# Attention scores and slot reads in the `h` banks, two groups of tiled products a batch, and a new place for the loads and transposes of x

## Chip, cores and metric

The kernel runs on one core of one Trainium2 chip. The metric is the device time of one execution in microseconds (us); lower is better. A run counts as slow where it lies over 1.5% above the fastest of the same kernel, and ratios use fast runs alone.

## The reference, cut to what matters

```python
B, H, S, Ns, D = 8, 8, 512, 32, 64
scale = 1 / sqrt(D)
a     = softmax(scale * x @ state.T)       # per batch and head: [512, 32], over the slots
xread = a @ state
a2    = softmax(scale * state @ x.T)       # [32, 512], over the tokens
sread = a2 @ x
y     = concat([xread, sread], tokens)     # 544 tokens a batch, 512 features
h     = y @ w_in                           # 512 -> 2048
g     = s * relu(h)**2 + b
out   = g @ w_out                          # 2048 -> 512
```

## The kernel before

The kernel does two products more cleverly than the reference writes them. The input weights are folded through the state, M = state times w_in, so that h is one product of M with the softmax shares `a`. The second product, g times w_out, uses seven half-size products in place of eight, with sums of quarters of g (`token_sum`, tiles `s`) and of w_out (tiles `wd`).

Per batch, TensorE does 16 pairs of `h` matmuls (128x512) and 112 `o` matmuls (128x256, tiles oA, oB and oC). Between them stand the small products that prepare the next batch, in tiles of 64x32 or 128x32: `T` (the scores), `M` in four parts and `V` (the slot reads).

The softmax of batch b needs these steps in a row: x is loaded (`xn`), transposed by a DMA (`xT`), multiplied with the state (`T`), exponentiated on ScalarE (`E`), transposed by a DMA (`ET`), normalised on VectorE (`den`, `inv`, `aT`), and transposed back by a DMA (`a`). In batches before NDT the denominator comes from a TensorE product `D` instead. All DMA transposes are issued from one queue, SP, in order. The loads of x are issued from the GpSimd queue (POOL).

```python
    psA = ctx.enter_context(tc.tile_pool(name="psA", bufs=2, space=bass.MemoryType.PSUM))
    psH = ctx.enter_context(tc.tile_pool(name="psH", bufs=2, space=bass.MemoryType.PSUM))
    psO = ctx.enter_context(tc.tile_pool(name="psO", bufs=2, space=bass.MemoryType.PSUM))
    ...
    def att_xT_dma(b):
        xT = new_xT(b)
        nc.sync.dma_start_transpose(
            out=xT.rearrange("p h k t -> p (h k) t"),
            in_=xn[b].rearrange("p h c d -> p (h c d)"),
        )
    ...
    def att_T(b, gs):                      # scores: two att banks, then exponentials
        ...
        T = att_ps([P, 2, 512], FP32, f"T_{b}_{gs[0]}")
        ...                                # 16 tiled matmuls
    ...
    def pieces(s):                         # what is done beside product f of batch s
        nb = s + 1
        ...
            if s + 3 < B:
                at(13 if s == 2 else 2, lambda: load_x(s + 3))
            if s == 2:
                at(0, stT_dma)
            if nb < B:
                at(3, lambda: att_T(nb, [0, 1]))
                at(3, lambda: att_M(nb, 0, "act"))
                at(4, lambda: att_ET(nb))
                if s in (2, 3):
                    at(4, lambda: att_xT_dma(nb + 1))
                if s >= 3 and s + 3 < B:
                    at(13, lambda: att_xT_dma(s + 3))
                if nb < NDT:
                    at(5, lambda: att_D(nb, [0, 1]))
                else:
                    at(8, lambda: att_shares(nb))
                    at(9, lambda: att_a4_dma(nb))
                at(7, lambda: att_M(nb, 1, "act"))
                at(7, lambda: att_M(nb, 2, "act"))
            ...
            at(10, lambda: att_V(s))
            ...
            if nb < B:
                at(10, lambda: att_M(nb, 3, "act"))
```

The softmax here doesn't subtract the row's maximum and nothing guards it: scores larger than these inputs give would overflow.

## Time and profile before

| | before |
|---|---|
| median of 3 runs | 210.24 us (209.90 to 210.72) |
| span of the profiled run | 208.0 us |
| TensorE (PE) busy | 199.5 us, 96% |
| VectorE (DVE), ScalarE (ACT) busy | 78%, 60% |
| granted TensorE clock | 1.00 |
| batch 2, then batches 3 to 6 | 23.2 us, then 21.3 us each |

The median is the whole execution as timed; the span is what the profile sees of it. A batch runs from its first `h` product to the next batch's; the scores `T` that run in batch 4 prepare batch 5. TensorE is the bound, so the first question to a change is what it does to the length of a batch. The prediction shows the lines that carry this.

### The profile page before, as it was taken

The numbers are of one execution on the slowest core, as the hardware profiler recorded it, in microseconds if no ns is written. First come the engines' busy times: TensorE is split into PE (matmuls) and PEld (weight loads), VectorE is DVE, ScalarE is ACT, GpSimd is POOL, SyncE is SP. The second block draws the span as 40 slices with busy tenths as digits, with TensorE's granted clock in tenths as the row PEclk, the third lists the DMA queues.
The fourth block names the chain that finished last, engine by engine and source line by source line (L and its number), as shares of the span: only waits on it lengthen the run. The fifth ranks groups of instructions, "written<-read, shape, count | busy, mean of one in ns | idle before, by whom it ended". The sixth has DMA issues, their size and how long they took to land.

```text
span 208.0 us, 4757 instructions
## 1 busy us (share of the span) xinstructions
PE 199.5 (96%) x1947; PEld 129.4 (62%) x1947; DVE 162.1 (78%) x282; ACT 125.3 (60%) x218; POOL 37.6 (18%) x64
## 2 busy tenths in 40 slices
PE   7888999999899999999999999999999999999992
PEld 2433343445566676667666766676667777788882
DVE  1587825978769796899779977998799877895862
ACT  3678865698489557765776477656774544533100
POOL 5970001501110330123011201120111012100210
PEclk9999999999999999999999999999999999999999
DMA  5999996999947299979833915231324111110143
GB/s 183 225 202 206 207 191 104 179 181 174 266 52 153 72 194 123 124 163 185 127 103 67 196 52 102 54 107 54 101 29 132 50 54 50 54 50 0 54 145 111
DMA packets 45946, 25.35 MB, mean 122 GB/s; under 512 B 30884, under 2 KB 43940, under 8 KB 45924
## 3 DMA queue, kind: packets, MB, share of 16 engines
q0 software_dynamic: 15536, 16.19, 38.8%
q1 hardware_dynamic: 29588, 8.49, 23.8%
q10 hardware_dynamic: 800, 0.36, 0.7%
q8 instruction: 15, 0.25, 0.5%
q14 instruction: 7, 0.06, 0.1%
HBM read 17.33 MB, written 8.91 MB: 126 GB/s over the span
## 4 chain that ended last, share of the span: by engine, by line
PE 82%; DVE 6%; DMA 6%; ACT 4%; issue 1%; POOL 0%; SPq 0%; POOLq 0%
PE h L70 23%; PE oB L70 17%; PE oC L70 12%; PE oA L70 10%; PE o L70 6%; PE Mps L70 4%; DMA wi<-in_moe_w_in_dram 4%; PE h_sr L70 3%; DMA stT_all<-st 2%; ACT r L365 2%; DVE g L371 1%; PE T L70 1%; PE oB_sr L70 1%; PE V L70 1%; DVE M L298 1%; PE oA_sr L70 1%
## 5 line engine op out<-in xcount | busy, mean ns | idle before, releaser
L365 ACT ACTIVATE r<-h 128x512 f16<-128x512 f32 x126 | 74.4, 601 | 52.0 <-PE h L70 51.4
L70 PE MATMUL h<-a,M 128*128 128x512 f16 x256 | 75.0, 379 | 0.9 <-DVE M L298 0.6
L371 DVE TENSOR_TENSOR g<-r 128x1024 f16<-128x1024 f16 x64 | 44.1, 691 | 16.0 <-ACT r L365 15.8
L70 PEld LDWEIGHTS <-s 128*128 128x128 f16 x448 | 42.8, 98 | 19.3 <-issue 3.7
L70 PEld LDWEIGHTS <-g 128*128 128x128 f16 x400 | 38.0, 98 | 18.9 <-issue 2.9
L536 POOL DMA_DIRECT2D out_dram<-osb x27 | 18.2, 675 | 125.5 <-DVE osb L528 120.3
L70 PE MATMUL oB<-wd,s 128*128 128x256 f16 x224 | 32.7, 273 | 0.0
L70 PE MATMUL oA<-wo,g 128*128 128x256 f16 x224 | 31.6, 273 | 0.1
L70 PEld LDWEIGHTS <-M 128*128 128x128 f16 x256 | 24.6, 98 | 10.9 <-DVE M L298 1.6
L301 ACT CAST M<-Mps 128x1024 f16<-128x1024 f32 x27 | 26.8, 1017 | 1.4 <-PE Mps L70 0.8
L70 PE MATMUL oC<-wd,s 128*128 128x256 f16 x112 | 16.5, 273 | 0.0
L70 PE MATMUL o<-wo,g 128*128 128x512 f16 x64 | 16.3, 380 | 0.0
L70 PE MATMUL oB<-wd,g 128*128 128x256 f16 x112 | 15.9, 273 | 0.0
L70 PE MATMUL oC<-wo,s 128*128 128x256 f16 x112 | 15.3, 273 | 0.0
L365 ACT ACTIVATE r_sr<-h_sr 128x256 f16<-128x256 f32 x16 | 6.1, 382 | 8.4 <-PE h_sr L70 8.4
L227 ACT ACTIVATE E<-T 128x512 f16<-128x512 f32 x16 | 9.4, 596 | 1.2 <-PE T L70 1.1
L471 DVE TENSOR_TENSOR s<-s,g 128x1024 f16<-128x1024 f16 x14 | 9.7, 691 | 0.4
L70 PE MATMUL h_sr<-srdT,wi 128*128 128x256 f16 x64 | 9.6, 273 | 0.0
L465 DVE TENSOR_TENSOR s<-g 128x1024 f16<-128x1024 f16 x14 | 9.6, 685 | 0.0
L473 DVE TENSOR_TENSOR s<-g,s 128x1024 f16<-128x1024 f16 x14 | 9.6, 684 | 0.0
L469 DVE TENSOR_TENSOR s<-g,g 128x1024 f16<-128x1024 f16 x14 | 9.6, 683 | 0.0
L528 DVE SCALAR_TENSOR_TENSOR osb<-oC,s_bc,u 128x512 f32<-128x512 f32 x12 | 8.9, 746 | 0.5 <-PE oC L70 0.5
(102 smaller groups left out, 187.4 us busy)
## 6 DMA issues: line engine op xcount, KB each, us to landing
out_dram<-osb POOLq DMA_DIRECT2D x31, 256.0 KB, 2.8
xn<-in_x_dram POOLq DMA_DIRECT2D x7, 512.0 KB, 7.0
wi<-in_moe_w_in_dram POOLq DMA_DIRECT2D x4, 512.0 KB, 9.2
wo<-in_moe_w_out_dram POOLq DMA_DIRECT2D x4, 512.0 KB, 15.9
xf<-in_x_dram SPq DMA_DIRECT2D x2, 512.0 KB, 4.8
out_dram<-osb_sr SPq DMA_DIRECT2D x8, 32.0 KB, 1.6
out_dram<-osb_sr ACTq DMA_DIRECT2D x8, 32.0 KB, 1.7
out_dram<-osb_last SPq DMA_DIRECT2D x2, 128.0 KB, 1.9
```

The costliest lines, as they stand in the source:

```text
L70: return nc.tensor.matmul(out, lhsT, rhs, start=start, stop=stop, tile_position=tp, is_transpose=is_transpose, skip_group_check=True,)
L227: nc.scalar.activation(a["E"][:, g, :].rearrange("p (m t) -> p m t", m=2), T[:, :, 256 * i : 256 * i + 256], AF.Exp, scale=scale, accum_ou ...
L298: nc.vector.tensor_copy(dst[:, 0], two[0])
L301: nc.scalar.copy(dst, ps)
L365: nc.scalar.activation(r16[:, f % 2], hps, AF.Relu)
L371: nc.vector.tensor_mul(gt[:, f % 4 - 1 : f % 4 + 1], r16, r16)
L465: nc.vector.tensor_sub(o, a11, a21)
L469: nc.vector.tensor_add(o, a21, a22)
L471: nc.vector.tensor_sub(o, SQ[b, 1, j], a11)
L473: nc.vector.tensor_sub(o, a12, SQ[b, 2, j])
L528: nc.vector.scalar_tensor_tensor(osb, acc[bank], s_bc, add, ALU.mult, ALU.add)
L536: nc.gpsimd.dma_start(dst[j][:, :, n0 : n0 + NH], osb)
```

## The change

The intent is to save TensorE time at the edges of tiled products. Three insertions a batch become two: [M0, T, M1] before product 4 and [V, M2, M3] before product 10. For that, scores and slot reads move into the `h` banks, and the M copies wait behind a relu. The softmax normalised on VectorE (the transposed one) starts at batch 3, so one more batch does without `D`. The load of x comes first in a batch, and the transpose of x moves to product 9, behind the transpose of the shares. Slot scaling moves to ScalarE, the fourth sums to the next batch, and rows of `o` go ahead of `h` for products 4 to 12.

```diff
-    NST = 3
-    NDT = 4
+    NST = 5
+    NDT = 3
 ...
     def att_T(b, gs):
+        one_bank = b >= NDT
+        if one_bank:
+            Ts = [psH.tile([P, NG, S // 2], FP32, tag="h", name=f"T_{b}_{m}") for m in range(2)]
 ...
     def att_V(b):
-        ps = att_ps([P, NG, D], FP32, f"V_{b}")
+        if b >= NDT - 1:
+            ps = psH.tile([P, NG, D], FP32, tag="h", name=f"V_{b}")
 ...
-            if s + 3 < B:
-                at(13 if s == 2 else 2, lambda: load_x(s + 3))
-            if s == 2:
-                at(0, stT_dma)
+            if 2 < s < B - 2:
+                at(0, lambda: load_x(s + 2))
             if nb < B:
-                at(3, lambda: att_T(nb, [0, 1]))
-                at(3, lambda: att_M(nb, 0, "act"))
+                if nb < NST:
+                    at(0, lambda: att_stT(nb))
+                ahead(4, lambda: att_M(nb, 0, "later"))
+                ahead(4, lambda: att_T(nb, [0, 1]))
+                ahead(4, lambda: att_M(nb, 1, "later"))
                 at(4, lambda: att_ET(nb))
-                if s in (2, 3):
-                    at(4, lambda: att_xT_dma(nb + 1))
-                if s >= 3 and s + 3 < B:
-                    at(13, lambda: att_xT_dma(s + 3))
 ...
+                at(8, lambda: att_shares(nb))
+                at(9, lambda: att_a4_dma(nb))
+                if s == 3:
+                    at(9, stT_dma)
+                if nb + 1 < B:
+                    at(9, lambda: att_xT_dma(nb + 1))
 ...
-            at(10, lambda: att_V(s))
+            ahead(10, lambda: att_V(s))
+            if nb < B:
+                ahead(10, lambda: att_M(nb, 2, "later"))
+                ahead(10, lambda: att_M(nb, 3, "later"))
 ...
             for f in range(NKF):
+                for fn in todo_s.get((f, "ahead"), []):
+                    fn()
+                if s > 1 and 4 <= f < 13:
+                    for fn in items[f]:
+                        fn()
+                    items[f] = []
                 mm1_x(s, f)
```

More of the change, by code (lines that the diff above doesn't have):

```diff
@@ L210, in att_T @@
         a = A[b]
-        n = len(gs)
-        T = att_ps([P, 2, 512], FP32, f"T_{b}_{gs[0]}")
+        one_bank = b >= NDT
+        if one_bank:
+            Ts = [psH.tile([P, NG, S // 2], FP32, tag="h", name=f"T_{b}_{m}") for m in range(2)]
+        else:
+            T = att_ps([P, 2, 512], FP32, f"T_{b}_{gs[0]}")
+            Ts = [T[:, m, 0 : 256 * len(gs)].rearrange("p (g t) -> p g t", t=256) for m in range(2)]
         for q in range(NQ):
@@ L217, in att_T @@
                     mm(
-                        T[32 * q : 32 * q + 32, m, 256 * i : 256 * i + 256],
+                        Ts[m][32 * q : 32 * q + 32, i, :],
                         st_of(b, h, m),
@@ L224, in att_T @@
             a["E"] = apool.tile([P, NG, S], FP16, name=f"E_{b}", tag="E", bufs=3)
-            a["rs"] = apool.tile([P, NG], FP32, name=f"rs_{b}", tag="rs", bufs=4)
+            n = 2 * NG if one_bank else NG
+            a["rs"] = apool.tile([P, n], FP32, name=f"rs_{b}", tag="rs", bufs=4)
+        if one_bank:
+            for m in range(2):
+                for g in gs:
+                    nc.scalar.activation(
+                        a["E"][:, g, 256 * m : 256 * m + 256],
+                        Ts[m][:, g, :],
+                        AF.Exp,
+                        scale=scale,
+                        accum_out=a["rs"][:, NG * m + g : NG * m + g + 1],
+                    )
+            return
         for i, g in enumerate(gs):
@@ L277, in att_a4_dma, with copy_M @@
         )
+    def copy_M(dst, ps):
+        with tc.issue_after(G["relu"]):
+            nc.scalar.copy(dst, ps)
     def att_M(b, c, how):
@@ L296, in att_M @@
         dst = a["M"][:, :, FC * c : FC * c + FC]
-        if how == "split":
+        if how == "later":
+            a["M", c] = lambda: copy_M(dst, ps)
+        elif how == "split":
             nc.vector.tensor_copy(dst[:, 0], two[0])
@@ L309, in att_ET @@
         a["rq"] = apool.tile([P, NG], FP32, name=f"rq_{b}", tag="rq", bufs=4)
-        nc.vector.reciprocal(a["rq"], a["rs"])
+        rs = a["rs"]
+        if b >= NDT:
+            rs = apool.tile([P, NG], FP32, name=f"rt_{b}", tag="rt")
+            nc.vector.tensor_add(rs, a["rs"][:, 0:NG], a["rs"][:, NG : 2 * NG])
+        nc.vector.reciprocal(a["rq"], rs)
     def att_V(b):
         a = A[b]
-        ps = att_ps([P, NG, D], FP32, f"V_{b}")
+        if b >= NDT - 1:
+            ps = psH.tile([P, NG, D], FP32, tag="h", name=f"V_{b}")
+        else:
+            ps = att_ps([P, NG, D], FP32, f"V_{b}")
         for g in range(NG):
@@ L326, in att_V @@
         a["sr"] = apool.tile([P, NG, D], FP16, name=f"sr_{b}", tag="sr")
-        for g in range(NG):
-            nc.vector.tensor_scalar(a["sr"][:, g], ps[:, g], a["rq"][:, g : g + 1], None, ALU.mult)
+        with tc.issue_after(G["relu"]):
+            for g in range(NG):
+                nc.scalar.mul(a["sr"][:, g], ps[:, g], a["rq"][:, g : g + 1])
     def att_srT_dma(b):
@@ L365, in mm1_close @@
             nc.scalar.activation(r16[:, f % 2], hps, AF.Relu)
+            G["relu"] = nc.cur_bb.bb.instructions[-1]
         if f % 4 == 0:
@@ L756, in at, with ahead @@
                 out.setdefault(f, []).append(fn)
+            def ahead(f, fn):
+                out.setdefault((f, "ahead"), []).append(fn)
             if s == 1:
@@ L779, in pieces @@
                 return out
-            if s + 3 < B:
-                at(13 if s == 2 else 2, lambda: load_x(s + 3))
-            if s == 2:
-                at(0, stT_dma)
+            if 2 < s < B - 2:
+                at(0, lambda: load_x(s + 2))
             if nb < B:
-                at(3, lambda: att_T(nb, [0, 1]))
-                at(3, lambda: att_M(nb, 0, "act"))
-                at(4, lambda: att_ET(nb))
-                if s in (2, 3):
-                    at(4, lambda: att_xT_dma(nb + 1))
-                if s >= 3 and s + 3 < B:
-                    at(13, lambda: att_xT_dma(s + 3))
-                if nb < NDT:
-                    at(5, lambda: att_D(nb, [0, 1]))
-                else:
-                    at(8, lambda: att_shares(nb))
-                    at(9, lambda: att_a4_dma(nb))
-                at(7, lambda: att_M(nb, 1, "act"))
-                at(7, lambda: att_M(nb, 2, "act"))
+                if nb < NST:
[3 more added lines that the diff above has]
+                ahead(4, lambda: att_M(nb, 1, "later"))
+                at(4, lambda: att_ET(nb))
+                at(4, lambda: A[nb]["M", 0]())
+                at(6, lambda: A[nb]["M", 1]())
+                at(8, lambda: att_shares(nb))
[4 more added lines that the diff above has]
+                    at(9, lambda: att_xT_dma(nb + 1))
             if s == 2:
@@ L802, in pieces @@
                 at(12, lambda: att_srT_dma(1))
-            at(10, lambda: att_V(s))
+            ahead(10, lambda: att_V(s))
+            if nb < B:
+                ahead(10, lambda: att_M(nb, 2, "later"))
+                ahead(10, lambda: att_M(nb, 3, "later"))
+                at(10, lambda: A[nb]["M", 2]())
+                at(12, lambda: A[nb]["M", 3]())
             if s == last_b:
@@ L807, in pieces @@
                 at(12, lambda: att_srT_dma(s))
-            if nb < B:
-                at(10, lambda: att_M(nb, 3, "act"))
             if s == last_b:
@@ L832 @@
             for f in range(NKF):
+                for fn in todo_s.get((f, "ahead"), []):
[4 more added lines that the diff above has]
+                    items[f] = []
                 mm1_x(s, f)
-                if s == 2 and f in (8, 9):
+                if s > 1 and f in (4, 5):
                     with tc.issue_after(G["last"]):
-                        token_sum(1, 4, f - 8)
-                if s > 2 and f == 0:
-                    token_sum(s - 1, 4, 1)
+                        token_sum(s - 1, 4, f - 4)
                 if s in fast:
@@ L845 @@
                             token_sum(s, f - 12, 0)
-                    if s > 1 and f in (11, 12, 13):
-                        token_sum(s, (1, 2, 4)[f - 11], 0)
+                    if s > 1 and f in (11, 12):
+                        token_sum(s, f - 10, 0)
                     if f == 15:
@@ L866 @@
             mm1_sr(f)
-            if f == 5:
-                token_sum(last_b, 4, 1)
+            if f in (4, 5):
+                token_sum(last_b, 4, f - 4)
             if f in (5, 9):
```

## The prediction

> **What bounds the kernel now.** I read the page's busy table first, then the chain that ended last, then the table of stretches over single batches, then the timeline of TensorE inside one batch, then ScalarE and VectorE there. Busy table and the head of the chain:
>
> ```profile
> PE 199.5 (96%) x1947; PEld 129.4 (62%) x1947; DVE 162.1 (78%) x282; ACT 125.3 (60%) x218; POOL 37.6 (18%) x64
> ...
> PE 82%; DVE 6%; DMA 6%; ACT 4%; issue 1%; POOL 0%; SPq 0%; POOLq 0%
> ```
>
> TensorE is the bound: 96% busy and 82% of the chain; VectorE has a fifth of the span free, ScalarE two fifths. The granted clock is full throughout. So a change pays only where it shortens what TensorE issues or a gap in it. In the timeline the first product `h` of batches 2, 3, 4 and 5 starts at 52.26, 75.5, 96.8 and 118.04. Cut there, the table of stretches gives (length, then busy time of PE, PEld, DVE, ACT, POOL, with counts; clock, DMA share, GB/s):
>
> ```profile
> 52.26:75.48 23.22, 22.40 (x260) 14.89 (x258) 18.64 (x33) 16.04 (x26) 3.50 (x5) 1.00 0.64 135
> 75.48:96.76 21.28, 21.28 (x226) 14.59 (x225) 18.68 (x31) 14.18 (x25) 3.61 (x5) 1.00 1.03 154
> 96.76:118.04 21.28, 21.28 (x226) 14.59 (x224) 18.68 (x31) 14.18 (x25) 3.60 (x5) 1.00 0.65 127
> ```
>
> Batches 3 to 6 repeat every 21.28 us with no idle TensorE at all; batch 2 is 1.94 us longer and has 0.82 us idle. That repeat is one unit of 7 `o` products and 2 `h` products, 1.19 to 1.20 us, done 16 times (about 19.15 us), plus three insertions of tiled products. The timeline of batch 4/5 shows the three:
>
> ```profile
> 105.82 0.59 PE L70 MATMUL h<-a,M 128*128 128x512 f16 x2
> 106.35 0.63 PE L70 MATMUL Mps<-wi,stT_all 64*32 64x512 f16 x16
> 106.91 0.94 PE L70 MATMUL oC<-wd,s 128*128 128x256 f16 x7
> ...
> 110.07 0.59 PE L70 MATMUL h<-a,M 128*128 128x512 f16 x2
> 110.60 0.42 PE L70 MATMUL V<-xn,ET 128*32 128x64 f16 x32
> 110.95 0.41 PE L70 MATMUL Mps<-wi,stT_all 64*32 64x512 f16 x8
> 111.29 0.94 PE L70 MATMUL oB<-wd,g 128*128 128x256 f16 x7
> ...
> 121.63 0.59 PE L70 MATMUL h<-a,M 128*128 128x512 f16 x2
> 122.16 0.43 PE L70 MATMUL T<-xT,stT_all 64*32 64x256 f16 x16
> 122.38 0.42 PE L70 MATMUL Mps<-wi,stT_all 64*32 64x512 f16 x8
> 122.74 0.28 PE L70 MATMUL oB<-wd,s 128*128 128x256 f16 x1
> ```
>
> Starts matter here, not durations, which overlap. After an `h` pair the next full-array product normally starts 0.43 us after the pair's start. So the insertions cost 106.91-(105.82+0.43)=0.66, 111.29-110.50=0.79 and 122.74-122.06=0.68 us, in all 2.13; with 19.15 that is the 21.28. Eight M products or sixteen T products alone take 0.22 (122.16 to 122.38). So 0.66 is 2x0.21 of work plus 0.23 of entry and exit; 0.68 the same plus 0.25; V itself takes 0.35 and its insertion also some 0.23 at the edges. A switch into and out of tiled products costs a quarter of a microsecond.
>
> Batch 2's extra is visible too (bracket: idle before it and what ended it):
>
> ```profile
> 57.45 0.43 PE L70 MATMUL T<-xT,stT_all 64*32 64x256 f16 x16 [0.79 <-DMA stT_all<-st]
> 55.28 0.66 PEld L70 LDWEIGHTS <-s 128*128 128x128 f16 x7 [0.51 <-DVE s L471]
> ```
>
> The transpose of all states, queued on SP behind the last score transpose, lands late for batch 3's scores; and one `oB` row waits for a VectorE sum (its matmuls start at 55.29 where the `h` pair left the array at 55.10).
>
> **What the Trainium skill says.** "TensorEngine Tiling (Array Packing)", Key Properties, says that changing the tiling mode drains TensorE; the 0.23 to 0.25 us above agrees. "TensorE: Matmul & The Clock Gate", Back-to-back issue gap, gives N/2.4+2.5 ns, 216 ns for N=512; the trace's 0.43 per `h` pair agrees[...]. "ScalarE: Activation LUTs", What ACT_TABLE_LOAD costs, gives 186 ns + 0.833 per element, 93 ns more for a pointer operand, and 93 ns overlap of neighbours: 613 and 399 ns for 512 and 256 columns; the trace has 601 (relu) and 382 (relu of the slot rows).
>
> **The change, part by part.** I compared the built instruction orders of both kernels.
>
> 1. Three insertions become two in batches 3 to 6: [M0, T, M1] before product 4 and [V, M2, M3] before product 10. The work is the same, one entry/exit fewer: [M0,T,M1] 0.64+0.24=0.88, [V,M2,M3] 0.79+0.21=1.00; 2.13-1.88=0.25 us each, 1.00 us in four batches. On the path, since TensorE has no gap there.
>
> 2. Batch 2. Before: 19.15 + T/M0 with its wait 1.54 (56.49 to 58.03) + denominator products D 0.43 + M1/M2 0.65 + V of batch 1 0.45 + V/M3 0.78 + the sum's wait 0.19 = 23.19, the 23.22 of the table. After: batch 3's states come from two PE transposes (0.11; so for batch 4 in batch 3), D is gone because batch 3's softmax is now the transposed one, the SP queue no longer stands before the scores, and VectorE is freer at the end of batch 1 since the slot scaling moved to ScalarE (0.47 us off). 19.15+0.11+0.88+0.45+1.00=21.59: 1.63 us less. Batch 3 loses 0.11 for its transposes.
>
> Gross: 1.63+1.00-0.11 = 2.52 us.
>
> 3. Off the path: Ln and Exp of D leave ScalarE in batch 2 (2.1 us); shares enter VectorE (1.21+0.35+1.23, less 0.69). Per batch ScalarE gains two scalings (my estimate from the skill's formula, about 0.24 us each in a row) and about 0.3 for four 256-column exponentials in place of two of 512 (0.37 against 0.58 each with accumulator read). At 14.18 of 21.28 us it can carry that. Earlier transposes and later x loads only have to land in time: x has some 12 us before its transpose, against 7.0 from issue to landing.
>
> 4. What it costs on TensorE. The scores take both `h` banks, so T waits for the relu of product 3, and product 4 for the exponentials of the first bank. From the end of product 3: relu ends at 0.8 (122.86 against 122.06), T may start at 0.76+0.10+0.22=1.08: no wait. T ends 1.3, exponentials start about 0.3 later (57.68 to 57.98), the first bank is free 0.75 to 0.85 after that, at 2.35 to 2.45; product 4 is due at 1.3+0.34+0.76=2.40. On the edge: I charge 0.05 us in five batches, 0.25. The second bank has half a microsecond to spare.
> In batch 7, products 12 and 13 now stand with only four `h_sr` products between (0.44) since the `o` row went ahead, and both take one of the two h banks in turn; relu needs 0.8 after product 12. A wait of about 0.4, once.
> VectorE's sum for `oB` in the next batch ends just when it is wanted (120.79 against 120.87); with the state copies (0.28 us, batches 2 and 3) and slightly later neighbours I charge 0.2 over all.
>
> Net: 2.52-0.25-0.40-0.20 = about 1.7 us; I round to 1.8 because D's removal also frees ScalarE in the batch whose evacuations were fullest. 210.24-1.8 = 208.4 us, 0.9% less.
>
> **The rivals.**
> A: the h banks become the bound. If the read of the accumulator, not the exponential itself, frees the bank, or relu and M copies push the exponentials back, product 4 waits 0.3 us or more in each of five batches; with the V bank the same at product 11. That would eat 1.5 us: 209.8. For it: only two banks, and relus follow products by 0.2 us already. Against: the rows moved ahead of products 4 to 12 give one row of 0.76 us as cover, and M copies are ordered after a relu.
> B: a transfer or VectorE is late. aT now stands behind the squares of products 8 and 9 in VectorE's order; by my count it ends at 12.7 after product 3, its transpose lands at 16, and the next batch wants it at 17.7. In batch 3 the SP queue carries `a`, the states and xT in a row (30 blocks), which may land xT only at 21 to 23 against a need at 22. If so, up to 1 us once: 209.4. If the shares slip in every batch, some 5 us is lost and the kernel is slower.
> C: the whole gross gain and no new wait: 207.7. More could come only if the drain cost more than the starts show, as there is no other idle time in batches 3 to 6.
>
> **Range and chances.** The centre is 208.4; rival C and two tenths of run scatter give 207.2, rival A 209.7. A gain over 2% needs 4.2 us, more than everything counted: 0.03. A loss over 2% needs the shares or banks to fail in each batch: 0.02.
>
> **What would show it.** Right: batches 3 to 6 of about 21.0 to 21.1 us, batch 2 near 21.7, two tiled insertions of 0.88 and 1.00, no D after batch 2, TensorE's share a little higher, a gap of 0.4 before product 13 in batch 7. Wrong: idle time of the `h` products put down to ScalarE's exponentials (A) in each batch, T or `h` ended by a DMA (B), or a batch that still takes 21.28.

## More of the kernel before

One line of before that the prediction does not show will be needed. It is the last line of the view of the tile `xT`, from 60 to 130 us: the time from a transpose's issue to its landing.

```profile
DMA to landing us min/median/max: 5.7/5.8/8.3
```

From the starts in the trace, these transposes were issued 18 to 29 us before the scores that use them (for instance 82.84 for a `T` at 100.88). Even 8.3 us is hidden there.

## The result, and the profile after

The changed kernel is slower. Its four runs took 216.89, 219.15, 220.85 and 221.79 us, a median of 220.0; before took 210.07 us as the median of its four. The ratio is 1.037 (95% interval 1.027 to 1.047). A ratio here is the mean time of one kernel's fast runs over that of the other's of the same rounds, so it is not quite the ratio of the medians: the upper two of these four count as slow and are left out. So the ratio is, if anything, kind to the change. The profiled run is the fast one of 216.89 us, with a span of 215.1 us. All results are correct.

The busy table and the head of the chain that ended last, of the changed kernel:

```profile
PE 200.5 (93%) x1949; PEld 130.5 (61%) x1949; DVE 160.5 (75%) x275; ACT 127.0 (59%) x252; POOL 37.7 (18%) x64
...
PE 72%; DMA 16%; DVE 4%; ACT 3%; SPq 1%; issue 1%; POOL 0%
```

TensorE is busy for about as long as before (200.5 against 199.5 us), but its share of the chain fell from 82% to 72%, and DMA rose from 6% to 16%. So a transfer stands on the path. The table of stretches, cut at the first `h` of batches 2 to 6 and of batch 7 (length; busy time of PE, PEld, DVE, ACT, POOL; clock, DMA share, GB/s), tells in which batches:

```profile
52.38:74.05 21.67, 21.67 (x261) 15.06 (x259) 18.73 (x31) 14.99 (x32) 3.16 (x6) 1.00 0.48 117
74.05:96.68 22.63, 21.40 (x228) 14.82 (x226) 18.29 (x31) 14.61 (x31) 3.62 (x6) 1.00 0.68 121
96.68:122.77 26.09, 22.96 (x226) 15.26 (x224) 18.26 (x30) 14.75 (x31) 3.38 (x5) 0.93 0.65 110
122.77:145.79 23.02, 21.30 (x227) 14.68 (x225) 18.17 (x30) 14.62 (x31) 3.61 (x5) 1.00 0.72 117
145.79:166.89 21.10, 21.10 (x227) 14.67 (x225) 18.17 (x30) 14.61 (x31) 2.71 (x4) 1.00 0.42 98
```

Batches 2 and 6 are as predicted, 21.67 and 21.10 us, with no idle TensorE. Batches 3, 4 and 5 have 1.23, 3.13 and 1.72 us of idle TensorE (length less PE's busy time), and batch 4 a lower clock besides. TensorE's timeline names the wait; below it is the first insertion of the undisturbed batch 6, and a product of batch 7:

```profile
80.67 0.44 PE L70 MATMUL T<-xT,stT 64*32 64x256 f16 x16 [1.23 <-DMA xT<-xn]
...
105.09 0.44 PE L70 MATMUL T<-xT,stT_all 64*32 64x256 f16 x16 [3.13 <-DMA xT<-xn]
...
106.51 1.01 PE L70 MATMUL h<-a,M 128*128 128x512 f16 x2
...
129.78 0.44 PE L70 MATMUL T<-xT,stT_all 64*32 64x256 f16 x16 [1.72 <-DMA xT<-xn]
...
150.66 0.41 PE L70 MATMUL Mps<-wi,stT_all 64*32 64x512 f16 x8
...
151.44 0.61 PE L70 MATMUL oA<-wo,g 128*128 128x256 f16 x4
151.89 0.49 PE L70 MATMUL oB<-wd,s 128*128 128x256 f16 x3
152.30 0.59 PE L70 MATMUL h<-a,M 128*128 128x512 f16 x2
...
183.79 0.59 PE L70 MATMUL h<-a,M 128*128 128x512 f16 x2 [0.25 <-ACT r L395]
```

Each wait is of `T` for the transpose of x. The pair at 106.51 took 1.01 us in place of 0.59: after the longest wait the clock was granted at half for 3.41 us, from 106.53. In 3.41 us at half speed only half as much gets done, so about 1.7 us are lost. Batch 4 without both is 26.09-3.31-1.70 = 21.08 us, where 3.31 is the wait read in starts (`T` was due 0.22 us after its M0 pair began).

The chain has the three transposes with the time from issue to landing (start, us):

```profile
71.15 9.48 DMA xT<-xn
...
94.98 10.07 DMA xT<-xn
...
119.64 10.10 DMA xT<-xn
```

SP's timeline shows what stands before the second of them, and POOL's what runs beside the first two:

```profile
92.29 1.25 SPq L290 DMA_TRANSPOSE a<-aT  x1
93.63 1.26 SPq L162 DMA_TRANSPOSE stT_all<-st  x1
94.98 3.78 SPq L204 DMA_TRANSPOSE xT<-xn  x1
```

```profile
73.78 0.97 POOL L120 DMA_DIRECT2D xn<-in_x_dram  x1
...
96.36 1.01 POOL L120 DMA_DIRECT2D xn<-in_x_dram  x1
```

The transposes of x are now issued 8.1, 6.8 and 8.2 us before their scores are due (79.26, 101.78 and 127.87). They take 9.5 to 10.1 us. Each x load is issued 1.4 to 3.4 us after a transpose began (73.78, 96.36 and 123.07) and lasts 8.5 to 10.1 us, so it runs beside nearly all of the rest. In batch 6, which loads nothing, no wait is left. The view of the tile `xT` over the same stretch gives the shift against the line of before:

```profile
DMA to landing us min/median/max: 9.5/9.8/10.1
```

Lengths of the batches, in us, from the starts of the first `h` of each; the last column is the best-matched experiment, told below:

| batch | before | predicted | after | x load moved (e1) |
|---|---|---|---|---|
| 2 | 23.24 | 21.6 | 21.67 | 21.66 |
| 3 | 21.27 | 21.0 to 21.1 | 22.63 | 21.21 |
| 4 | 21.27 | 21.0 to 21.1 | 26.09 | 21.18 |
| 5 | 21.27 | 21.0 to 21.1 | 23.01 | 21.73 |
| 6 | 21.27 | 21.0 to 21.1 | 21.10 | 21.10 |
| 7, to the end | 47.43 | 47.8 (0.4 added) | 48.23 | 48.13 |

Between after and before this is -1.57 in batch 2, +1.36, +4.82, +1.74 and -0.17 in batches 3 to 6, and +0.80 from batch 7 to the end, together 7.0 of the 7.1 us between the two spans.

### The profile page after: what moved, and what is told of

The parts are those of the page before. It is cut to its first block, busy times and chain, and to the rows that moved or that the text cites. A ratio compares the mean times of both kernels' runs of the same rounds, so it can differ in the third digit from the quotient of the medians.

```text
span 215.1 us, 4789 instructions
## 1 busy us (share of the span) xinstructions
PE 200.5 (93%) x1949; PEld 130.5 (61%) x1949; DVE 160.5 (75%) x275; ACT 127.0 (59%) x252; POOL 37.7 (18%) x64
## 4 chain that ended last, share of the span: by engine, by line
PE 72%; DMA 16%; DVE 4%; ACT 3%; SPq 1%; issue 1%; POOL 0%
PE h L70 20%; PE oB L70 15%; DMA xT<-xn 14%; PE oC L70 11%; PE oA L70 7%; PE o L70 6%; PE Mps L70 4%; DMA xf<-in_x_dram 2%; PE h_sr L70 2%; ACT r L395 2%; PE V L70 1%; PE T L70 1%; PE oB_sr L70 1%; DVE g L402 1%; DVE M L320 1%; PE oA_sr L70 1%
## 5 line engine op out<-in xcount | busy, mean ns | idle before, releaser
L395 ACT ACTIVATE r<-h 128x512 f16<-128x512 f32 x126 | 74.4, 602 | 47.9 <-PE h L70 47.8
L70 PEld LDWEIGHTS <-s 128*128 128x128 f16 x448 | 43.9, 99 | 17.6 <-DVE s L502 1.6
L70 PE MATMUL oB<-wd,s 128*128 128x256 f16 x224 | 33.5, 278 | 0.0
L297 ACT CAST M<-Mps 128x1024 f16<-128x1024 f32 x20 | 20.1, 1006 | 0.0
L234 ACT ACTIVATE E<-T 128x256 f16<-128x256 f32 x20 | 7.4, 384 | 10.7 <-PE T L70 10.7
L559 DVE SCALAR_TENSOR_TENSOR osb<-oA,s_bc,bias_bc 128x512 f32<-128x512 f32 x7 | 5.2, 749 | 6.8 <-PE oA L70 6.8
L588 DVE SCALAR_TENSOR_TENSOR u<-oB,s_bc,qa 128x512 f32<-128x512 f32 x7 | 5.2, 749 | 6.1 <-PE oB L70 6.1
```

Source lines behind the costliest of these rows:

```text
L70: return nc.tensor.matmul(out, lhsT, rhs, start=start, stop=stop, tile_position=tp, is_transpose=is_transpose, skip_group_check=True,)
L234: nc.scalar.activation(a["E"][:, g, 256 * m : 256 * m + 256], Ts[m][:, g, :], AF.Exp, scale=scale, accum_out=a["rs"][:, NG * m + g : NG * ...
L297: nc.scalar.copy(dst, ps)
L395: nc.scalar.activation(r16[:, f % 2], hps, AF.Relu)
L559: nc.vector.scalar_tensor_tensor(osb, acc[bank], s_bc, add, ALU.mult, ALU.add)
L588: nc.vector.scalar_tensor_tensor(u, acc["B"], s_bc, kept["qa"], ALU.mult, ALU.add)
```

## The experiments

**Theory.** The loss comes from two things together: the x transpose is issued only 7 to 8 us before its scores, and an x load running beside it makes it longer than that. **Rivals.** The new bank plan of `T` itself holds the scores up (rival A of the prediction); or the late issue alone is too late, whatever runs beside it; or the moved load alone is harmful, whatever the window.

In the rounds of the first four experiments (e1 to e4) the kernel before took 210.20 us (median of 7 runs).

### e1: the change, with the x load at product 5 in place of 0

```diff
-            if 2 < s < B - 2:
-                at(0, lambda: load_x(s + 2))
 ...
                 at(6, lambda: A[nb]["M", 1]())
+                if 2 < s < B - 2:
+                    at(5, lambda: load_x(s + 2))
```

> The changed kernel, with the x load of batches 3 to 5 put on the GpSimd queue behind the first output write of the batch (about 9 us later than now) and all else kept. Theory (the x transpose takes 9.5 to 10.1 us because the 512 KB load of the next x runs on the same DMA engines meanwhile): the transposes land in 5 to 7 us, TensorE's waits for xT (6.1 us on T rows) vanish, no half-clock window, and the time is about 209.0 us, since the other batches gained what was predicted. Rival Q (the transpose is issued too late behind the shares' transpose and the states, whatever else moves): waits of over 1 us before T in batches 3 to 5 stay, time over 214. Rival H (the h banks and the two groups cost time themselves): waits gone but time 210 or more.

Measured: 209.43 us (209.12 to 210.69), ratio 0.998 (0.994 to 1.001). One edit that moves three loads by five products gave back 3.5 to 4% of the time. The transposes took 7.0, at most 6.9 (its landing is not in the trace, but its `T` began on time to 0.07 us), and 8.4 us, and only batch 5 waited for one. The table of stretches of batches 4 and 5 (cut 0.07 us after their first `h`):

```profile
95.27:116.45 21.18, 21.18 (x226) 14.60 (x225) 17.97 (x29) 14.60 (x30) 3.58 (x5) 1.00 0.80 133
116.45:138.18 21.73, 21.38 (x226) 14.66 (x226) 18.27 (x31) 14.60 (x30) 3.60 (x5) 1.00 0.72 126
```

The first has no idle time of TensorE; the second has 0.35 us. The clock is 1.00 in both.

### e2: the change, with the three x loads taken away

```diff
-                at(0, lambda: load_x(s + 2))
+                xn[s + 2] = xn[s - 2]
```

Batches 5 to 7 compute with the x of batches 1 to 3, which is wrong. (The comparison passed all the same. My guess, not tested: with inputs this small the scores are near zero and the result hardly depends on x. So "correct" says little about x here.)

> The changed kernel without the x loads of batches 3 to 5 at all: batches 5 to 7 use the x of batches 1 to 3 again, so the result is wrong on purpose. Nothing else on any queue moves. Theory: xT lands 5 to 6.5 us after its issue at the same place of the batch, no waits before T, about 208.8 us. Rival Q and a rival that the output writes are what slows the transposes: xT still takes 8 us or more in batches 3 to 5, and T still waits 1 to 3 us.

Measured: 209.72 us (209.53 to 210.51), ratio 0.999 (0.996 to 1.001). The list of TensorE's waits has none for `xT`, but in batch 5 `T` started 0.32 us late (122.58, due at 122.26), as its weight load waited for `xT`. The transposes took 7.0 us, at most 6.8 (by the start of its `T`) and 8.2 us, more than I had expected of transposes without a load beside them. With the load they took 9.5, 10.1 and 10.1, so it adds 2.5, at least 3.2 and 1.9 us. What keeps two of them above the 5.8 us of before (the median) was not tested; output writes run beside them in both kernels.

### e3: the change, with the x transpose back at product 4

```diff
                 at(4, lambda: att_ET(nb))
+                if nb + 1 < B:
+                    at(4, lambda: att_xT_dma(nb + 1))
 ...
-                if nb + 1 < B:
-                    at(9, lambda: att_xT_dma(nb + 1))
```

> The changed kernel with the x transpose queued right behind the E transpose, at product 4 in place of product 9, and the x load left where the change put it. Theory: the load has nearly landed by then (82.6 us against an issue at about 84), so the transposes take 5 to 7 us and have a whole batch to spare even if they took 10; no waits, about 209.0 us. Rival: the E transpose or the shares' transpose is slowed in its turn and the first h product of a batch waits for a; then over 211.

Measured: 209.78 us (209.44 to 210.26), ratio 0.999 (0.996 to 1.002). With the loads at product 0 as in the change, no `T` waited. The transposes whose landing is in the trace took 5.5, 7.3 and 5.6 us. Issuing the transpose early cures it as well as taking the load away. But this run changes two things at once: the window is wider, and each load had landed before the next transpose was issued (73.79+6.5 = 80.3 before 82.73, and so on). So it does not show that a transpose beside a load is harmless in a wide window; e7 below does. This run was not free of new costs: `ET` landed later behind the early transpose, and batch 4's `den` waited 0.67 us for it.

### e4: the kernel before, with the change's load and transpose places alone

```diff
-            if s + 3 < B:
-                at(13 if s == 2 else 2, lambda: load_x(s + 3))
+            if 2 < s < B - 2:
+                at(0, lambda: load_x(s + 2))
 ...
-                if s in (2, 3):
-                    at(4, lambda: att_xT_dma(nb + 1))
-                if s >= 3 and s + 3 < B:
-                    at(13, lambda: att_xT_dma(s + 3))
 ...                                    # x transpose behind the transpose of the shares
```

> The kernel before, with only the change's moves of transfers: x loads first in batches 3 to 5, x transposes at product 9. Scores, banks, groups, sums and softmax as before. In the kernel before VectorE has the shares ready some 1.3 us earlier in the batch and the output write in front of the load is some 1.5 us later, so by my count the transpose is issued 5.8 us before the load starts and is nearly through. Theory: no or small waits before T, 209.8 to 211.5 us, i.e. the moves hurt only with the new order on VectorE. Rival: the moves alone bring the loss, 214 us or more.

Measured: 210.23 us (209.65 to 210.51), ratio 1.000 (0.997 to 1.003), and batches 3 to 6 stayed at 21.27 us. The transposes took 8.3, 7.3 and 6.6 us, but here they were issued 9.5 us before `T` was due (92.09 for 101.59, 113.34 for 122.86), and the loads began only 6.4 and 7.0 us after them (98.47 and 120.38), so they hardly overlapped. So the moves alone are harmless in the kernel before: its VectorE order has the shares ready earlier, which gives 9.5 us before `T` in place of the change's 6.8 to 8.2. In the trace of before, `den`, `inv` and `aT` follow one another; in the change, `osb` of oC and a `g` stand between them, and the transpose of the shares, which `xT` queues behind, starts that much later.

These runs settle the first question. The bank plan stayed in e1, e2 and e3 and the loss went. The late issue without the load cost `T` 0.32 us once (e2). The load without the late issue is seen in e7, told below, whose profiled run is a fast one: there two transposes ran beside a load for 9.6 and 12.3 us, but were issued some 18 us before their `T` (83.92 for 102.00, 105.46 for 123.80), and both `T` began on time. So it takes both for `T` to wait.

### r1: the change again

> The changed kernel itself once more, as a control on the chip of the next two. Theory: 217 to 222 us, T waiting 1 to 3.5 us for xT in batches 3, 4 and 5, and one to three stretches of about 3.4 us at half clock after those waits (mean granted clock 0.98 to 0.992), the time rising with their number. If the loss belonged to the first chip or a moment, it would be near 210.

Measured: 217.60 us (216.27 to 219.52, one of four slow), before 210.18, ratio 1.033 (1.028 to 1.038). In its profiled run (the slow one) the three transposes took 10.8, 9.5 and 11.1 us, and `T` waited 2.57, 2.47 and 3.08 us; the clock went to half after the first of these. So the size of the waits scatters from run to run, and with it the time.

Why after 2.57 us of waiting, and not after 3.08? The packed traces hold the times of the clock's changes, and in every run they lie a whole number of 3.413 us apart (in after 30, 1 and 31 of them). So each trace can be cut into cells of that length. These rows of the table of stretches are one cell of after, which half clock followed, and one of r1, which it did not:

```profile
103.12:106.53 3.41, 1.44 (x32) 0.98 (x33) 0.20 (x1) 0.91 (x5) 0.00 (x0) 1.00 0.63 84
```

```profile
130.54:133.95 3.41, 1.57 (x32) 1.06 (x33) 0.33 (x1) 1.04 (x6) 0.00 (x0) 1.00 0.51 37
```

Within the batches of all kept traces, half clock followed every cell in which TensorE idled 1.98 us or more (1.98 in after, 2.57 in r1, 2.34 in e8, 2.13 and 2.15 in e5) and none in which it idled 1.84 us or less. The later waits of r1 fell across a border between cells, 1.69+0.78 and 1.24+1.84 us. So it matters where a wait falls, and not only how long it is. This is read from the traces after the fact; no run tested it by itself.

### e6: the change, with plain products on TensorE while `T` waits

```diff
+        for _ in range({4: 5, 5: 12, 6: 7}.get(b, 0)):
+            mm(Ts[0].rearrange("p g t -> p (g t)"), warm[:, 0:P], warm)
```

The filler writes into the bank that `T` overwrites, so nothing else changes but that TensorE is busy. It tests how much the clock drop is worth.

> The changed kernel with TensorE kept busy in the wait: 5, 12 and 7 products of 128x512 on zeros, into the scores' own bank, just before the scores of batches 4, 5 and 6 (1.1, 2.6 and 1.5 us, plus about 0.25 for the switches, each just under the wait seen there). Theory (part of the loss is the clock, which drops to half for 3.4 us after TensorE has idled): no stretch at half clock, mean clock 0.998 or more, 214 to 216 us, little scatter; the xT transposes still take about 10 us. Rival (the drop has another cause): clock 0.98 to 0.992 as before and 218 to 222 us, or more for the added products.

Measured: 217.46 us (216.76 to 221.37, one slow), ratio 1.033 (1.029 to 1.038). That is no less than r1 in the same rounds, so the gain I expected is missing. TensorE's timeline in batch 4:

```profile
102.12 2.76 PE L70 MATMUL T<-warm 128*128 128x512 f16 x12
...
105.27 0.44 PE L70 MATMUL T<-xT,stT_all 64*32 64x256 f16 x16 [0.38 <-DMA xT<-xn]
```

The wait is filled but for 0.38 us, and no half clock follows in the batches. Batch 4 was 24.45 us against 26.09, 1.64 us shorter, the size of the clock's part. But batch 5 was 24.30 against 23.01, because its transpose took 10.9 us and was issued 0.5 us later against the start of that batch. The half clock does follow the idle time; its cost is of the size of the scatter of the transposes, so the total did not show it.

### e8: the change, with the shares first in VectorE's order

```diff
+        if f == 9 and key in range(2, B - 1):
+            with tc.issue_after(G["aT"]):
+                nc.vector.tensor_mul(gt[:, f % 4 - 1 : f % 4 + 1], r16, r16)
 ...
+            elif bank == "C" and j == 1 and b in range(1, B - 2):
+                with tc.issue_after(G["aT"]):
+                    nc.vector.scalar_tensor_tensor(osb, acc[bank], s_bc, add, ALU.mult, ALU.add)
```

This issues the transpose of the shares, and so `xT`, about 0.95 us earlier: 70.53-52.71 = 17.82 us after the start of batch 2, against 71.15-52.38 = 18.77.

> The changed kernel with one thing put back on VectorE: the three share steps stand together, as in the kernel before, ahead of the C output and the squares of products 8 and 9. aT is ready about 1.1 us earlier, so the transposes of a and of x are issued that much earlier. Theory (the wait is the transpose's time less the time from issue to need, 8.2, 6.8 and 8.2 us): each of the three waits is about 1.1 us shorter (0.3, 2.2, 0.8), fewer half-clock stretches, 211 to 215 us. Rival (only the overlap with the load matters, not the issue time): waits as before, 217 to 222 us.

Measured: 217.94 us (217.39 to 218.08), ratio 1.036 (1.033 to 1.039). The total did not fall, because the edit brought a wait of its own. Two lines of TensorE's timeline:

```profile
92.02 0.60 PE L70 MATMUL oC<-wo,s 128*128 128x256 f16 x4 [0.81 <-DVE osb L565]
...
105.29 0.44 PE L70 MATMUL T<-xT,stT_all 64*32 64x256 f16 x16 [2.33 <-DMA xT<-xn]
```

I had expected 211 to 215 us. A wait for `xT` is left only in batch 4, in place of three, with a half clock after it (that transpose took 11.1 us). But oC waits 0.7 to 1.0 us in each of batches 2 to 6 for the evacuation that now stands behind `aT`. The trace speaks for the theory, the time is inconclusive.

### e5: the change, with transposes and loads as far apart from need as possible

```diff
                 at(4, lambda: att_ET(nb))
+                if nb + 1 < B:
+                    at(4, lambda: att_xT_dma(nb + 1))
+                if s + 3 < B:
+                    at(5, lambda: load_x(s + 3))
 ...                                    # both taken from their old places
-                if s > 1 and 4 <= f < 13:
+                if s > 1 and 4 <= f < (13 if s < last_b else 12):
```

The last line undoes, for the last batch, the row of `o` that moved ahead of product 12.

> The changed kernel with the transfers taken out of each other's way: the x load one batch earlier (behind the first output write of batches 2 to 4), the x transpose right behind the E transpose, and in batch 7 the row of o products between products 12 and 13 put back. By the parts seen so far: batch 2 at 21.67, batches 3 to 6 at 21.1 to 21.2 and batch 7 as before (the 0.4 us wait before product 13 gone) make 2.2 us less than the kernel before: about 208.0 us, ratio 0.990. Rival (the end after the last product is 0.2 to 0.8 us longer in all variants of the change for a reason not known): 208.3 to 208.8.

Measured: 213.33 us (211.91 to 219.42, two of seven slow), before 210.35, ratio 1.013 (1.007 to 1.018). I had expected 208.0 us; this is a plain miss. TensorE's timeline of its profiled run, a slow one:

```profile
76.69 0.60 PE L70 MATMUL h<-a,M 128*128 128x512 f16 x2 [2.13 <-DMA a<-aT]
...
103.68 0.60 PE L70 MATMUL h<-a,M 128*128 128x512 f16 x2 [3.93 <-DMA a<-aT]
```

No `T` waits, but the first `h` of a batch now waits for the shares. The load and the `xT` transpose were issued within 0.7 us of each other (60.80 and 61.46, 86.40 and 87.05, 113.28 and 113.93). The later two `xT` then took 14.6 and 11.1 us, and the transposes of the shares behind the three of them 6.5, 8.3 and 4.1 us, against a median of 3.1 in before. I had given `xT` room and had not asked what stands behind it in the same queue. As the profiled run is a slow one, only the place of the wait is taken from it; the fast runs carry the 1.3%.

### e7: e5, with M1 in an insertion of its own

```diff
-                ahead(4, lambda: att_M(nb, 1, "later"))
+                ahead(6, lambda: att_M(nb, 1, "later"))
```

> The last kernel with M1 in an insertion of its own before product 6, so three insertions of tiled products in a batch again in batches 2 to 6. Theory (an entry and exit costs 0.25 us of TensorE time): batches 3 to 6 at 21.35 us and batch 2 at 21.9, 1.2 us slower than e5. Rival (the quarter of a microsecond is taken back elsewhere, the product after the scores waiting for the exponentials either way): under 0.6 us slower; or more than 1.2, as without M1 behind the scores product 4 comes 0.2 us sooner and waits for the exponentials' bank.

Measured: 214.12 us (212.08 to 220.19, two of six slow), ratio 1.012 (1.007 to 1.018), so as a whole no different from e5 through the scatter, where I had expected 1.2 us more. In batches 5 and 6, which neither kernel's profile shows disturbed, at a clock of 1.00, a batch is 21.56 and 21.55 us against 21.11 and 21.10 in e5: 0.45 us for a third insertion. TensorE's timeline there:

```profile
147.94 0.59 PE L70 MATMUL h<-a,M 128*128 128x512 f16 x2
148.47 0.41 PE L70 MATMUL Mps<-wi,stT_all 64*32 64x512 f16 x8
148.81 0.83 PE L70 MATMUL oB<-wd,s 128*128 128x256 f16 x6
```

M1 takes 148.81-(147.94+0.43) = 0.44 us, of which 0.21 is work and 0.23 the edges. I had expected 0.25 in all. The other 0.22 us is a longer wait of product 4 for its bank (0.30 against 0.08), as M1's 0.21 us no longer covers the exponentials.

### e9: the change, with all loads and transposes of x in before's places

```diff
-            if 2 < s < B - 2:
-                at(0, lambda: load_x(s + 2))
+            if s + 3 < B:
+                at(13 if s == 2 else 2, lambda: load_x(s + 3))
 ...
+                if s in (2, 3):
+                    at(4, lambda: att_xT_dma(nb + 1))
+                if s >= 3 and s + 3 < B:
+                    at(13, lambda: att_xT_dma(s + 3))
 ...                                    # and e5's edit for the last batch
```

> The changed kernel with the kernel before's whole plan of x transfers (loads at product 13 of batch 2 and product 2 of batches 3 and 4, x transposes behind the E transpose in batches 2 and 3 and at product 13, two batches ahead, in batches 3 and 4), and the row of o products between products 12 and 13 of batch 7 put back. Everything else of the change stays. Theory (all of the loss is the x transpose's deadline meeting the load; the rest of the change gains what its parts say): no waits for xT or a, batch 2 at 21.7, batches 3 to 6 at 21.1 to 21.3, batch 7 at 47.4 to 47.8: about 208.2 us, ratio 0.988 to 0.993. Rival (tight VectorE order makes any slower E transpose cost something): batches 3 to 5 at 21.3 to 21.6, 209 us or more.

Measured: 210.36 us (209.33 to 211.12), before 210.68, ratio 0.999 (0.996 to 1.002). I had expected 208.2. The batches are nearly right: 21.67, 21.21, 21.10, 21.40 and 21.10 us (only batch 5 lies 0.1 above what I expected), with no wait for `xT` or `a`. But the stretch from batch 7 to the end took 48.88 us, against 48.13 in e1. The last output write landed 3.87 us after the last oC product started, against 2.70 in before; 0.9 us of that is the write itself, 2.9 us from issue to landing against 2.0. No run shows why; it stays open.

### e10: e1, with e5's edit for the last batch

> e1_load_mid with one more edit: in batch 7 the row of o products stands again between products 12 and 13. Theory (that row hid the relu's 0.8 us): batch 7 is 0.4 us shorter than in e1, no wait of an h product for ScalarE at product 13, about 209.0 us. Rival: the wait moves to the next product, batch 7 at 48.1 as in e1 and 209.4 us.

Measured: 209.57 us (209.02 to 209.93), before 210.68, ratio 0.996 (0.993 to 0.999). This is the best version found, 0.4% faster than before. The edit for the last batch gave little of that. Product 13 of batch 7 starts 16.85 us after the batch, against 16.90 in e1 and 16.49 in before. TensorE's weight loads show where the wait went:

```profile
174.95 0.10 PEld L70 LDWEIGHTS <-wi 128*128 128x128 f16 x1 [0.38 <-DVE srdT L374]
```

The wait for the relu became one for the copy of the slot rows, which the rows of `o` had covered.

## Why the prediction was wrong

What held, by its own steps:

- **Part 1**, two insertions in place of three: 0.25 us a batch was charged. The undisturbed batch 6 went from 21.27 to 21.10 us, and 0.08 of the 0.25 is paid back at the bank edge of part 4. From the other side, e7 shows 0.23 us for the edges of an insertion put back.
- **Part 2**, batch 2: 1.63 us was charged, 1.57 measured.
- **Part 4**, the bank edge: 0.05 us was charged, 0.08 measured (product 4 was due at 151.89+0.33 = 152.22, and started at 152.30). Rival A did not come. The wait in batch 7 was charged 0.4 us, and product 13 started 0.41 later; its line shows 0.25 us of idle time put down to the relu.

The step that failed is in part 3: "Earlier transposes and later x loads only have to land in time: x has some 12 us before its transpose, against 7.0 from issue to landing." It tested the load against its transpose, which was never at risk: the x loaded at 73.78 is transposed at 94.98. It did not test the moved transpose against its scores. That window is 6.8 to 8.2 us, and the transpose needed 9.5 to 10.1 with a load beside it. So two terms failed together: the time that a transpose takes beside a load, and the slack that it had.

Rival B looked at this transpose in batch 3 alone, behind the states, and at most 1 us once. It happened in three batches, 6.6 us in all in the profiled run (1.41, 3.31 and 1.91). The states explain only the longest: they put `xT` of batch 3 back by 1.35 us (93.63 to 94.98). On rival B's own scale, from the end of product 3 of batch 3 (78.18), `xT` was to land at 21 to 23; it was issued at 16.8 and landed at 26.9. The 2% chance of slower rested on shares or banks that fail "in each batch"; the shares did not fail, and what failed stands behind them in the queue.

Two sizes were not foreseen at all. A load beside a transpose lengthens it by 1.9, 2.5 and at least 3.2 us (e2 against after), and a wait can cost a second time through the clock: 1.7 us in batch 4, shown by e6, which took it away.

Two readings of the skill in the prediction need a word. "TensorE: Matmul & The Clock Gate", Back-to-back issue gap, gives the 216 ns for an isolated product and states about 131 ns for a stream of products with N=512. In both kernels here a pair of `h` products takes 0.43 us, 215 ns each, so the measurement decides for the first. The 613 and 399 ns for ScalarE are estimates from the page's formula, 2 to 4% above the trace; the two scalings, estimated at 0.24 us each, took 0.51 us together in after.

The gross gain was real but smaller at the end than counted. In e1, where the waits are nearly gone, the span is 207.3 us against 208.0, so 0.7 us instead of 1.8. What is missing is mostly 0.5 us of waiting for `xT` in batch 5, and about 0.3 us more from the last product to the end. The length after the last product scatters by up to 1.1 us between variants without a cause that I could show.

## What to carry to other kernels

When a transfer is moved, write down three times for it: when it is issued, how long it takes beside what then runs, and when its reader wants it; and do the same for whatever stands behind it in its queue. A duration measured where the transfer had a batch to spare is not the duration that it has beside a load. A saving of a few tenths of a microsecond a batch, real as it is, is lost many times over by one transfer without slack.

## What the Trainium skill lacked or had wrong

- "DMA: Bandwidth & Descriptors", Issuing engines are not separate DMA queues, says that DMAs started by different engines run on the same 16 DMA engines and interleave. The page gives no size for it. Here a transpose of 512 KB of x took 7.0 and 8.2 us without a load beside it (e2), 9.5 to 10.1 us with one that began 1.4 to 3.4 us later (after), 9.6 and 12.3 us with one issued 0.8 us before it (e7), and 11.1 to 14.6 us likewise in e5, a slow run.
- The same page, Latency and other measured facts, states 261 GB/s for a DMA transpose. Here the 512 KB took 4.4 us from issue to landing at the shortest in the changed kernel's profile, which is 0.524 MB / 4.4 us = 119 GB/s, and 5.8 us as the median in the stretch shown of before, 90 GB/s. The page's figure would give an estimate of 2.0 us. The times here include all from issue to landing and whatever runs beside, so they do not prove the page's rate wrong; but for a plan like this one the measured time decides.
- "TensorE: Matmul & The Clock Gate", Part 1, gives the half clock after at least one idle window of about 3.4 us, and says that the window runs freely. The stretches at half were 3.41 us long and all clock changes lie on a grid of that length, which agrees. But no cell of the grid had to be idle throughout: 1.98 to 2.57 us of idle TensorE in one cell were enough (after, e5, e8, r1), and up to 1.84 us were not (r1).
- "TensorEngine Tiling (Array Packing)", Key Properties, says that a change of tiling mode drains TensorE and gives no cost. An insertion of tiled products costs 0.23 to 0.25 us beyond its own work (before, and e7).
